# A new order of work for a sketched-attention kernel: PSUM banks named per operation, rows turned from PSUM

## The chip, the cores and the metric

The kernel runs on one core of a Trainium2 chip. A core has five engines, each with its own list of instructions in a fixed order: TensorE (PE, matrix products, with the loading of weights shown apart as PEld), VectorE (DVE), ScalarE (ACT), GpSimd (POOL) and SyncE (SP, which here only issues DMAs). They work side by side and wait for each other by semaphores. Data lies in SBUF (128 partitions); TensorE writes to PSUM (128 partitions, eight banks of 512 fp32 each). The metric is the device time in microseconds (us); lower is better. The kernel before takes 122.55 us, the median of three runs (122.51 to 123.03).

## The reference

Attention with sketched features, without a softmax, then a small network on each token. There are 4 batches, 4 heads, 1088 tokens and 32 elements per head:

```python
def phi(x):                       # 32 elements -> 8 x 8 = 64 features
    a = np.einsum('rd,bhsd->bhsr', S1, x)
    b = np.einsum('rd,bhsd->bhsr', S2, x)
    return np.einsum('bhsi,bhsj->bhsij', a, b).reshape(*x.shape[:-1], r * r)
q_p, k_p = phi(q), phi(k)
kv  = einsum('bhsf,bhsd->bhfd', k_p, v);  z = sum(k_p, axis=2)
num = einsum('bhsf,bhfd->bhsd', q_p, kv)
den = einsum('bhsf,bhf->bhs', q_p, z)[..., None] + 1e-06
x   = (num / den) laid out as (batch, token, 128)
xn  = (x - mean(x)) / sqrt(var(x) + 1e-06) * g_ln
out = x + maximum(xn @ w_ch1, 0) @ w_ch2          # 128 -> 512 -> 128
```

q, k, v are fp32; `S1`, `S2`, `g_ln`, `w_ch1` and `w_ch2` arrive as the 64-bit words of doubles and are turned to fp32 on the chip.

## The kernel before, in words

The order of everything is written by hand. `PROGRAM` is one string of operations with arguments; each calls a small function that issues one or a few instructions. What stands ahead in the string stands ahead on its engine too; waits between engines are put in from the data. A letter names the engine where there is a choice: V is DVE, A is ACT, G is POOL, S is SP. So `relu A B 0 2 2 4` is: ACT, PSUM bank B, chunk 0, slice 2 of the 512 hidden columns, token tiles 2 to 4.

PSUM is held in six tiles: two of two banks (X and Y, whose halves are A, B and C, D) and M, N, O, K of one bank each. Several operations always use the same one: `k_sum`, `k_sc`, `k_val`, `k_spr` use K, the packed features and the numerators use X and Y.

*Weights* (`w_ex` … `w_mul`, index 0 for S, 1 for w1, 2 for w2). Exponent, mantissa and sign of the double words are put together to fp32 by some eight elementwise steps, on DVE, ACT and POOL as the letter says. w1 goes in halves of 256 columns, w2 in one piece of 512. `fold` multiplies w1 by a matrix that centres and scales by `g_ln`, so that the product with x needs no mean; 1/sqrt(var) is applied at the end.

*Keys of a batch.* `ld S k b` loads them; `turn_g`, `turn_r` turn them on DVE so that elements lie on partitions. The features come directly as tokens by features (`k_dir`, nine 128x128 products, batches 0 and 1) or packed by features on partitions (`k_feat`) and are then turned by DVE (`k_tok`). `k_prod` forms the 64 products, `k_sum`, `k_zs`, `k_sc`, `k_sccp` the sums for the denominators; `k_val` multiplies by v (72 small products), and `k_vcp`, `k_spr`, `k_rcp` bring the result to the form that `num` needs.

*Queries of a batch.* Batch 0's are loaded in pieces by head and tokens (`ld_t`, `ld_tr`), turned by PE (`turn_p`) and copied (`turn_c`); `q_dir` gives features and denominators at once. Batches 1 to 3 use `turn_g`, `q_feat` and two `q_tok`. Then `q_ac`, `q_den`, `q_rec` (denominator and its reciprocal), `q_a2`, `q_prod` (64 products) and `q_turn` (DVE). In batch 0 the products read the features from PSUM (`q_ac0`, `q_b0`, `q_prod0`). All batches share one buffer of products for keys (`kp`), one for queries (`qp`) and one for turned query products (`qpT`).

*Rows and the network.* `num` (packed 32x32 products) gives the numerators with features on partitions, `num_cp` copies them to SBUF as `xT`: chunks 2b and 2b+1 of 512 tokens for batch b, and the 64 tokens over in chunks 8 (batches 0, 1) and 9 (batches 2, 3). `hid` (one of four slices of the hidden layer for 512 tokens), `relu` and `sec` (one tile of 128 tokens, four products) run on these. For statistics and the residual the rows are also needed with tokens on partitions: chunks 0, 1, 8 and 9 are turned by PE (`row_pe`, `row_cp`); chunks 2 to 7 by DVE in blocks of 32 (`row_turn`, one call per chunk, from the copy in SBUF), written to DRAM (`row_wr`) and read back in rows (`row_rd`). `st_bn`, `st_ag`, `st_pow` give 1/sqrt(var). At the end either DVE scales the `sec` and adds x in one instruction (`fin`), or ACT scales (`fin_a`, four tiles per call) and POOL adds (`fin_g`); `store` and `store_r` write to DRAM.

Line numbers that the views name, before: 254 `fill` (empty products that keep PE busy), 421 `turn_g`, 439 `turn_r`, 445 `turn_p`, 463 `k_dir`, 481 `k_feat`, 505 `k_sum`, 534 `k_val`, 569 `q_dir`, 602 `q_feat`, 611 `q_tok`, 649 `q_turn`, 663 `num`, 715 `row_pe`, 725 `row_turn`, 745 `st_bn`, 772 `hid`, 780 and 782 `relu`, 788 `sec`, 801 `fin`, 807 `fin_a`, 817 `fin_g`; 82, 84 and 87 are the helpers for copies and products, which many operations share.

Of the kernel before, what the change touches and what calls it, by code (L numbers as in the profile page):

```python
# [25 lines left out]
def kernel(  # L26
# [40 lines left out]
    XS = [ps.tile([P, 1024], F32, name=f"X{i}") for i in range(2)]  # L67
    M = [ps.tile([P, 512], F32, name=f"M{i}") for i in range(2)]
    PO = ps.tile([P, 512], F32, name="PO")
    KV = ps.tile([P, 512], F32, name="KV")  # L70
    banks = {"X": XS[0], "Y": XS[1], "M": M[0], "N": M[1], "O": PO, "K": KV,
             "A": XS[0][:, 0:512], "B": XS[0][:, 512:1024],
             "C": XS[1][:, 0:512], "D": XS[1][:, 512:1024]}

# [40 lines left out]
    @op  # L115
    def ld(eng, x, b, t0, t1):
        dst, src = rows_in[x]
        by[eng].dma_start(
            out=dst[b][:, D * t0 : D * t1],
            in_=bass.AP(src.tensor, src.offset + b * H * S * D + D * t0,  # L120
                        [[G * D, P], [1, D * (t1 - t0)]]),
        )

    @op
    def ld_u(eng, x, b, u0, u1):
        dst, src = rows_in[x]
# [315 lines left out]
    def turn_p(z, u0, u1):  # L442
        for u in range(u0, u1):
            n = P if u < 8 else 64
            pe.transpose(banks[z][:, P * (u - u0) : P * (u - u0) + n],
                         qt[0:n, P * u : P * (u + 1)], ident[0:n, 0:n])

    @op
    def turn_c(eng, z, u0, u1):
        n = P * (u1 - u0) - (64 if u1 == 9 else 0)  # L450
        copy(eng, qT[0][:, P * u0 : P * u0 + n], banks[z][:, 0:n])
# [9 lines left out]
    def k_dir(b, u0, u1, z):  # L461
        for u in range(u0, u1):
            pe.matmul(banks[z][:, KW * (u - u0) : KW * (u - u0 + 1)],  # L463
# [3 lines left out]
    def k_cp(eng, b, u0, u1, z):  # L467
        copy(eng, kf[b % 2][:, KW * u0 : KW * u1], banks[z][:, 0 : KW * (u1 - u0)])

    @op  # L470
    def k_prod0(u0, u1, z, k0):
        f, n, o = kf[0], (u1 - u0) * H, KW * (u0 - k0)
        times("V", _ap(kp, 0, P, H * F * u0, [[F, n], [R, R], [1, R]]),
              _ap(banks[z], 0, P, o, [[2 * R, n], [2, R], [0, R]]),
# [3 lines left out]
    def k_feat(b):  # L478
        for g in range(4):
            for hp in range(2):  # L480
                pe.matmul(
                    XS[0][32 * g : 32 * g + 32, 512 * hp : 512 * hp + TW],
# [6 lines left out]
    def k_tok(b):  # L489
        dve.transpose(_ap(kf[b % 2], 0, P, 0, [[32, 2], [KW, NU], [1, 32]]),  # L490
                      _ap(XS[0], 0, P, 0, [[512, 2], [32, NU], [1, 32]]))
# [9 lines left out]
    def k_sum(b):  # L501
        f = kf[b % 2]
        for u in range(NU):
            c = u % 4
            pe.matmul(
                KV[32 * c : 32 * c + 32, 128:160], _ap(f, 0, P, KW * u + 1, [[2, HR]]),
# [5 lines left out]
    def k_zs(b):  # L512
        dve.tensor_tensor(out=_ap(zT, 0, P, 0, [[R, H], [1, R]]),
                          in0=_ap(KV, 0, P, 128, [[R, H], [1, R]]),
# [15 lines left out]
    @op  # L530
    def k_val(b):
        for u in range(NU):
            for h in range(H):
                pe.matmul(
                    KV[D * h : D * h + D, 0:F],
# [6 lines left out]
    def k_vcp(eng, b):  # L542
        copy(eng, _ap(kvc, 0, P, 0, [[P, 2], [32, 4], [1, 32]]),
             _ap(KV, 0, P, 0, [[32, 2], [0, 4], [1, 32]]))

    @op
    def k_spr(b):
        for i in range(2):
            pe.transpose(KV[:, 256 + P * i : 256 + P * (i + 1)], kvc[:, P * i : P * (i + 1)], ident)

    @op
    def k_rcp(eng, b):
        copy(eng, kvr[b % 2], KV[:, 256:512])
# [13 lines left out]
    def q_dir(u0, u1, z):  # L567
        for u in range(u0, u1):
            pe.matmul(banks[z][:, W0 * (u - u0) : W0 * (u - u0 + 1)], qT[0][:, P * u : P * (u + 1)],
# [382 lines left out]
```

## Time and profile before

| | |
|---|---|
| median of three runs | 122.55 us (122.51 to 123.03) |
| span of the profiled execution | 120.9 us, 1.6 below the median |
| busy PE / PEld / DVE / ACT / POOL | 108.4 / 78.6 / 84.0 / 38.7 / 48.4 us |
| DMA | 13.31 MB: 9.31 read, 3.80 written |
| mean granted clock of PE | 0.993 |

The span runs from the first to the last instruction; the run times are measured from outside and also hold what lies around them. The views that follow give times in us from the span's start. In a group (`L421 DVE STREAM_TRANSPOSE qT<-qn 128x1024 …`) stand the line, the engine, the operation, the output and input tile with partitions x elements and the count; then the busy time of all, the mean of one in ns, and the idle time before them with what ended it. A table by stage gives busy time and number of instructions of PE, PEld, DVE, ACT and POOL for each stretch, then granted clock, share of DMA time and GB/s. The chain that ended last gives start, duration, engine, tile and line of each piece.

### The profile page before, as it was taken

The numbers are of one execution on the slowest core, as the hardware profiler recorded it, in microseconds if no ns is written. First come the engines' busy times: TensorE is split into PE (matmuls) and PEld (weight loads), VectorE is DVE, ScalarE is ACT, GpSimd is POOL, SyncE is SP. The second block draws the span as 40 slices with busy tenths as digits, with TensorE's granted clock in tenths as the row PEclk, the third lists the DMA queues.
The fourth block names the chain that finished last, engine by engine and source line by source line (L and its number), as shares of the span: only waits on it lengthen the run. The fifth ranks groups of instructions, "written<-read, shape, count | busy, mean of one in ns | idle before, by whom it ended". The sixth has DMA issues, their size and how long they took to land.

```text
span 120.9 us, 3295 instructions
## 1 busy us (share of the span) xinstructions
PE 108.4 (90%) x1347; PEld 78.6 (65%) x1347; DVE 84.0 (69%) x229; ACT 38.7 (32%) x100; POOL 48.4 (40%) x64
## 2 busy tenths in 40 slices
PE   5993999999898998998999799999979979979970
PEld 3382999848766773874665589766237946549970
DVE  2953308249999799899788999885993655391550
ACT  0062124224334358030701820264491500414000
POOL 6502242035839963301587903339643500006100
PEclk9999999999999999999999999999999999999997
DMA  3999799996000023011640120013640225300423
GB/s 110 262 315 245 139 251 233 272 249 182 0 5 5 0 62 131 0 26 68 203 147 0 43 87 0 5 66 118 188 159 0 87 92 173 91 17 13 161 87 108
DMA packets 15502, 13.31 MB, mean 110 GB/s; under 512 B 6528, under 2 KB 12416, under 8 KB 15488
## 3 DMA queue, kind: packets, MB, share of 16 engines
q1 hardware_dynamic: 11744, 9.54, 28.5%
q10 hardware_dynamic: 3712, 3.57, 9.7%
q8 instruction: 10, 0.16, 0.6%
q14 instruction: 4, 0.03, 0.1%
q0 software_dynamic: 32, 0.00, 0.0%
HBM read 9.31 MB, written 3.80 MB: 108 GB/s over the span
## 4 chain that ended last, share of the span: by engine, by line
PE 57%; DVE 18%; DMA 8%; ACT 6%; issue 4%; POOL 2%; ACTq 1%; DVEq 0%; POOLq 0%
PE X L772 8%; PE M L788 7%; PE X L663 5%; PE M L772 5%; DMA kn<-in_k_dram 4%; PE X L788 4%; DVE xh L725 4%; PE KV L788 3%; PE X L463 3%; DVE qpT L649 3%; DMA w_raw<-in_moe_w_ch_dram 3%; PE PO L788 3%; PE PO L772 2%; ACT xT L82 2%; PE M L463 2%
## 5 line engine op out<-in xcount | busy, mean ns | idle before, releaser
L758 POOL TENSOR_TENSOR rstd<-va,mhalf 128x4 f32<-128x4 f32 (+1 forms) x10 | 10.2, 1024 | 29.1 <-DVE va L752 28.1
L788 PEld LDWEIGHTS M<-w,hT 128*128 128x128 f32 x144 | 17.1, 192 | 5.1 <-issue 2.4
L788 PE MATMUL M<-w,hT 128*128 128x128 f32 x144 | 18.4, 278 | 1.1 <-ACT ob L807 0.6
L772 PE MATMUL X<-xT,w 128*128 128x512 f32 (+1 forms) x38 | 18.4, 586 | 0.8 <-DVE xr L84 0.8
L780 ACT ACTIVATE hT<-X 128x512 f32<-128x512 f32 (+2 forms) x18 | 9.9, 556 | 21.3 <-PE X L772 19.8
L87 POOL TENSOR_TENSOR kp<-kf 128x1280 f32<-128x1280 f32 (+3 forms) x7 | 13.1, 1883 | 4.9 <-ACT kf L82 3.2
L87 POOL TENSOR_TENSOR qp<-a,fq 128x1280 f32<-128x1280 f32 (+1 forms) x4 | 9.6, 2398 | 5.1 <-DVE a L87 5.0
L649 DVE STREAM_TRANSPOSE qpT<-qp 128x1280 f32<-128x1280 f32 (+2 forms) x9 | 11.0, 1227 | 0.5 <-POOL qp L87 0.4
L82 ACT COPY xT<-X 128x256 f32<-128x256 f32 (+1 forms) x13 | 6.1, 510 | 15.9 <-PE X L663 11.5
L772 PE MATMUL M<-xT,w 128*128 128x512 f32 (+1 forms) x20 | 9.0, 532 | 1.4 <-DVE hT L782 0.9
L254 PE MATMUL M<-ones 128*128 128x128 f32 (+2 forms) x16 | 8.7, 696 | 1.4 <-DVE m L202 1.4
L772 PEld LDWEIGHTS X<-xT,w 128*128 128x128 f32 x38 | 6.3, 190 | 4.7 <-issue 4.2
L663 PE MATMUL X<-qpT,kvr 32*32 32x288 f32 (+2 forms) x384 | 7.9, 332 | 1.1 <-issue 0.5
L725 DVE STREAM_TRANSPOSE xh<-xT 128x512 f32<-128x512 f32 x6 | 6.5, 1102 | 0.9 <-ACT xT L82 0.9
L772 PEld LDWEIGHTS M<-xT,w 128*128 128x128 f32 x20 | 3.4, 189 | 5.5 <-issue 1.9
L663 PEld LDWEIGHTS X<-qpT,kvr 32*32 32x32 f32 x384 | 4.7, 103 | 3.0 <-issue 1.0
L745 DVE BATCH_NORM_STATS2 st<-x 128x6 f32<-128x128 f32 x32 | 6.7, 274 | 0.0
L788 PEld LDWEIGHTS X<-w,hT 128*128 128x128 f32 x48 | 5.9, 192 | 1.0 <-issue 1.0
L788 PEld LDWEIGHTS KV<-w,hT 128*128 128x128 f32 x40 | 4.9, 191 | 2.2 <-ACT hT L780 1.7
L788 PE MATMUL X<-w,hT 128*128 128x128 f32 x48 | 6.2, 275 | 0.0
L772 PE MATMUL PO<-xT,w 128*128 128x512 f32 (+1 forms) x14 | 6.2, 522 | 0.0
L817 POOL TENSOR_TENSOR ob<-ob,x 128x512 f32<-128x512 f32 x4 | 5.1, 1282 | 2.5 <-ACT ob L807 2.5
(164 smaller groups left out, 195.2 us busy)
## 6 DMA issues: line engine op xcount, KB each, us to landing
out_dram<-ob SPq DMA_DIRECT2D x7, 256.0 KB, 2.9
vn<-in_v_dram SPq DMA_DIRECT2D x13, 128.0 KB, 4.8
qn<-in_q_dram SPq DMA_DIRECT2D x3, 544.0 KB, 5.6
xd<-xh SPq DMA_DIRECT2D x5, 256.0 KB, 2.3
kn<-in_k_dram ACTq DMA_DIRECT2D x2, 544.0 KB, 6.3
x<-xd SPq DMA_DIRECT2D x4, 256.0 KB, 2.7
kn<-in_k_dram SPq DMA_DIRECT2D x1, 544.0 KB, 7.5
w_raw<-in_moe_w_ch_dram SPq DMA_DIRECT2D x1, 512.0 KB, 6.3
```

Of the source, the lines that this page charges most:

```text
L82: act.copy(o, i)
L87: by[eng].tensor_tensor(out=o, in0=a, in1=b, op=ALU.mult)
L254: pe.matmul(M[0][:, 0:w], ones[:, 0:P], ones[:, 0:w], start=True, stop=True)
L463: pe.matmul(banks[z][:, KW * (u - u0) : KW * (u - u0 + 1)], kT[b % 2][:, P * u : P * (u + 1)], sk0, start=True, stop=True)
L649: dve.transpose(_ap(qpT, 0, P, 32 * u0, [[32, u1 - u0], [TW, 8], [1, 32]]), qp[:, H * F * u0 : H * F * u1])
L663: pe.matmul(XS[r // 2][D * h : D * h + D, o : o + w], kvr[b % 2][rows, DM * f + D * h : DM * f + D * h + D], qpT[rows, c : c + w], start=( ...
L725: dve.transpose(_ap(xh[slot(c)], 0, P, 0, [[32 * n, 4], [32, n], [1, 32]]), _ap(cols(c), 0, P, 0, [[1, 4], [P, n], [4, 32]]))
L745: dve.bn_stats(out=sts[slot(c)][:, 6 * t : 6 * t + 6], in_=row_ap(c, t))
L758: pool.tensor_tensor(out=rstds[slot(c)][:, 0:n], in0=vas[slot(c)][:, 0:n], in1=mhalf[:, 0:n], op=ALU.pow)
L772: pe.matmul(banks[z][:, 0:n], w1[:, P * j : P * (j + 1)], cols(c)[:, a : a + n], start=True, stop=True)
L780: act.activation(o, i, AF.Relu)
L788: pe.matmul(banks[z][:, DM * t : DM * (t + 1)], h[:, 512 * j + P * t : 512 * j + P * (t + 1)], w2[:, DM * j : DM * (j + 1)], start=(j == 0 ...
```

## The change

It does seven things.

1. PSUM is one tile of eight banks, and every operation names its bank or banks in `PROGRAM`.
2. Batch 0's features are direct, all others packed: batch 1's keys go through `k_feat` and `k_tok`. In batch 0's queries, `q_cp` now copies all 24 columns to SBUF, and the products are made from there, most of them on POOL, with the functions of the other batches.
3. `num` of batch 0 comes in two calls instead of three, and its columns lie as those of the other batches; `store` follows.
4. All of chunks 0 to 7 are turned by DVE and go through DRAM, each in two calls that read the numerators from PSUM instead of `xT`. PE turns chunks 8 and 9 alone.
5. k has two buffers instead of four, q two instead of three beside batch 0's.
6. `fin_a` takes one tile per call: 20 tiles go by `fin_a`, 14 by `fin`.
7. The order on all engines is new. Among others: `ld S q 1` and `turn_g q 1` stand ahead of the second half of `turn_g k 0`; w2 is loaded with w1 and converted mostly by ACT and POOL; `hid` of chunk 9 stands after the last `sec` of chunk 7.

```diff
-    XS = [ps.tile([P, 1024], F32, name=f"X{i}") for i in range(2)]
...
+    ALL = ps.tile([P, 4096], F32, name="ALL")
+    def bank(z, c0=0, c1=512):
+        return ALL[:, 512 * z + c0 : 512 * z + c1]
+    def pair(z, off, free):
+        return _ap(ALL, 0, P, 512 * z[0] + off, [[512 * (z[1] - z[0]), 2]] + free)
-    kn = const([P, G * D], F32, "kn", B)
+    kn = const([P, G * D], F32, "kn", 2) * 2
+    NAT = True
+    QDIR = {0}
+    qb = const([P, G * D], F32, "qn", 2)
+    qn = [qt, qb[0], qb[1], qb[0]]
     def num_cp(eng, b, i, u0, u1, *z):
-        o, w, r = (64 * i, 1, 32) if b == 0 else (2 * i, 4, 1)
+        copy(eng, _ap(xT[(2 * b + u0 // 4) % 4], 0, P, P * (u0 % 4) + 2 * i,
+                      [[1, 2], [P, n], [4, 32]]),
+             pair(z, 32 * u0, [[32, n], [1, 32]]))
-    through_dram = set((2, 3, 4, 5, 6, 7, ))
+    through_dram = {0, 1, 2, 3, 4, 5, 6, 7}
-    def row_turn(c):
+    def row_turn(c, i, *z):
         n = tiles(c)
-        dve.transpose(_ap(xh[slot(c)], 0, P, 0, [[32 * n, 4], [32, n], [1, 32]]),
-                      _ap(cols(c), 0, P, 0, [[1, 4], [P, n], [4, 32]]))
+        dve.transpose(_ap(xh[slot(c)], 0, P, 64 * n * i, [[32 * n, 2], [32, n], [1, 32]]),
+                      pair(z, P * (c % 2), [[32, n], [1, 32]]))
-    def fin_a(z, c):
-        for t in range(tiles(c)):
-            act.activation(...)
+    def fin_a(z, c, t):
+        act.activation(...)
-        runs = [[8 * DM, P]] if b == 0 else [[G * DM, 32], [8 * DM, 4]]
+        runs = [[8 * DM, 32], [256 * DM, 4]] if b == 0 and NAT else [[G * DM, 32], [8 * DM, 4]]
     PROGRAM = """
+    ld_s A 1; ld_s A 0; c_iota; c_ones; fill 4 256 7; c_small; ld A k 0 0 16; c_masks;
...
+    ld_t A 0 0 4; ld_w S 1 0 2; ld A k 0 16 34; w_low A 1 0 256; w_ex V 1 256 512;
...
+    s_heads G; turn_g k 0 0 2; ld_g; turn_r k 0; ld S q 1 0 34; turn_g q 1 0 4; ld_w S 2 0 4;
+    turn_g k 0 2 4; c_vpad 1; sk 6; sk_0 6; fill 1 256 7; k_dir 0 3 6 5; ld_t S 0 4 8;
...
+    sk_8 6; c_vpad 3; ld_v S 1 3; ld_v S 1 1; ld S k 2 0 34; sk_2 6; w_exf A 1 0 256; ld_v S 0 0;
+    c_pads 0; k_dir 0 6 9 4; ld_t S 3 0 4; ld_t A 2 4 8; ld_tr S; turn_r k 1; turn_p 3 0 4;
...
+    k_sccp A 0 1; c_rest; ld_t S 3 4 8; turn_p 7 4 8; q_dir 0 4 3; ld S k 3 0 34; turn_c A 7 4 8;
+    turn_c A 2 8 9; c_cg G; ld_vr S 0 0; q_cp A 0 4 3 0 24; q_ac G 0 0 4; q_dir 4 9 7;
...
+    k_sum 2 7; q_a2 G 0 0 4; q_prod G 0 0 2; q_a2 G 0 4 9; q_prod V 0 2 4; q_prod G 0 6 9;
+    q_turn 0 2; k_spr 0 3; q_prod G 0 4 6; q_feat 1 5 6 1 2; k_zs 2 7; q_turn 2 4; q_tok 1 0 5 6;
+    ld_vr S 1 0; k_rcp A 0 3; ld_vr S 2 0; q_turn 4 9; k_prod G 1 0 5; q_tok 1 1 1 2; turn_r k 3;
...
+    w_mant A 2 0 512; num 0 0 4 3 4 5 6; q_ac V 1 0 4; q_ac V 1 4 9; num_cp A 0 0 0 4 3 4;
+    k_feat 3 1 2; k_prod G 1 5 9; k_val 1 0 9 7; q_den 1 0 4; num_cp A 0 1 0 4 5 6;
+    hid 0 0 0 2 4; q_den 1 4 9; ld_vr S 3 0; q_rec 1 0 4; k_vcp A 1 7; q_rec 1 4 9; k_tok 3 1 2;
+    row_turn 0 1 5 6; ld_v S 3 0; hid 2 0 1 2 4; relu A 0 0 0 2 4; q_a2 G 1 0 4;
...
+    relu A 1 1 2 0 4; k_val 2 0 9 7; row_wr S 0; k_vcp A 2 7; row_wr S 1; w_e2 G 2 0 512;
+    k_sum 3 3; q_turn 4 9; q_ac G 2 0 4; ld_vr S 3 1; w_e3 V 2 0 512; w_add G 2 0 512;
+    relu A 4 1 0 0 4; row_rd S 0; k_zs 3 3; num 1 0 9 5 6 0 1; k_spr 2 7; k_sc 3 3;
+    relu V 2 0 1 0 2; hid 4 1 3 0 4; ld_v S 3 1; w_mul G 2 0 512; sec 2 0 1; st_bn 0;
...
+    sec 6 2 2; hid 3 3 0 0 4; k_vcp V 3 7; q_ac G 3 0 4; q_ac G 3 4 9; k_spr 3 7;
+    row_turn 4 1 4 5; sec 2 2 1; st_ag 3; num_cp A 2 0 0 4 0 1; row_turn 5 0 0 1; num_r V 2 0 1;
+    fin_g G 1; num_cp V 2 0 4 8 0 1; k_rcp V 3 7; relu A 3 3 0 0 4; store S 0 0 4; sec 7 2 0;
...
+    st_bn 7; fin 1 6 1; sec 1 7 1; sec 4 7 2; fin 5 6 3; sec 5 7 3; row_pe 9 2; st_ag 7;
+    st_pow 7; fin 0 6 0; hid 0 9 0 0 1; fin 6 6 2; fin 4 7 2; store S 6 0 4; fin 7 7 0;
+    hid 7 9 1 0 1; fin 1 7 1; row_cp A 9 2; fin 5 7 3; relu A 7 9 1 0 1; store S 5 0 4;
...
```

More of the change, by code (lines that the diff above doesn't have):

```diff
@@ L883 @@
-    row_rd S 2; fin_g G 0; relu A O 2 2 0 4; turn_g q 2 0 4; turn_g q 3 0 4; k_zs 3; q_feat 2;
-    hid N 3 0 0 4; sec M 1 1; k_spr 2; q_tok 2 1; q_tok 2 0; st_bn 1; st_ag 1; k_prod G 3 0 5;
-    sk_qq 3; c_vpad 3; st_pow 1; hid D 3 1 0 4; relu V D 3 1 0 4; hid B 2 0 0 4; q_ac V 2 4 9;
-    q_den 2 4 9; q_rec 2 4 9; q_a2 G 2 4 9; hid K 8 2 0 1; hid D 2 3 0 4; st_bn 3; q_ac G 2 0 4;
-    q_den 2 0 4; q_prod G 2 4 9; relu A B 2 0 0 4; hid B 8 1 0 1; hid C 3 2 0 4; k_sc 3;
-    k_sccp V 3; q_rec 2 0 4; relu A D 2 3 0 4; fin_a M 1; hid O 3 3 0 4; sec M 2 0; ld_v A 3 0;
@@ L889 @@
-    relu A C 3 2 0 4; q_a2 V 2 0 4; st_bn 2; relu A B 8 1 0 1; sec M 2 3; q_feat 3;
-    relu A O 3 3 0 4; relu A N 3 0 0 4; q_prod V 2 0 4; q_turn 4 9; q_tok 3 0; relu V K 8 2 0 1;
-    k_rcp V 2; hid N 8 0 0 1; relu V N 8 0 0 1; q_tok 3 1; q_turn 0 4; sec O 3 1; sec O 3 2;
-    sec M 2 2; sec M 2 1; hid K 8 3 0 1; sec O 3 0; num 2 0 9; ld_v S 3 2; sec O 3 3;
-    num_cp A 2 1 4 8; num_r A 2; relu A K 8 3 0 1; fin_g G 1; q_ac G 3 0 4; q_ac G 3 4 9;
-    store S 1 0 4; num_cp A 2 0 0 4; k_prod V 3 5 9; q_den 3 4 9; q_rec 3 4 9; st_ag 3; st_ag 2;
```

292 lines of the change are left out of this document (131 added, 161 removed).

## The prediction

> **What bounds the kernel now.** I read, in this order: the page's busy line, busy time by stage, the chain that ended last, the groups of instructions, the timeline of DVE and POOL. The stages (start:end, length; busy time of PE, PEld, DVE, ACT, POOL; granted clock, DMA share, GB/s):
>
> ```profile
> PE 108.4 (90%) x1347; PEld 78.6 (65%) x1347; DVE 84.0 (69%) x229; ACT 38.7 (32%) x100; POOL 48.4 (40%) x64
> 0.00:11.41 11.41, 8.11 (x18) 4.55 (x18) 5.51 (x26) 2.78 (x6) 3.61 (x19) 1.00 0.83 236
> 11.41:28.41 17.00, 17.00 (x182) 14.62 (x183) 7.42 (x20) 4.10 (x13) 4.74 (x12) 1.00 1.03 231
> 28.41:42.00 13.59, 12.72 (x359) 9.75 (x358) 13.05 (x24) 5.91 (x17) 10.75 (x9) 1.00 0.06 18
> 42.00:57.50 15.50, 14.48 (x234) 9.73 (x214) 14.51 (x32) 5.89 (x14) 5.17 (x3) 1.00 0.17 57
> 57.50:77.70 20.20, 19.51 (x245) 13.75 (x245) 18.33 (x49) 6.09 (x16) 10.78 (x13) 1.00 0.23 72
> 77.70:117.30 39.60, 36.63 (x334) 26.23 (x332) 24.83 (x83) 13.96 (x34) 13.34 (x12) 1.00 0.28 96
> ```
>
> PE looks full everywhere, but its records overlap. DVE tells the stages apart: until 28.4 the loads set the pace (DMA share 0.83 to 1.03, DVE under half busy); from 28.4 to 77.7 DVE is busy 45.9 of 49.3 us and paces everything; after 77.7 DVE is free a third of the time and PE paces. What PE really needs is read from the chain, whose pieces do not overlap (start, us, work):
>
> ```profile
> 4.96 5.39 DMA kn<-in_k_dram
> 11.41 1.54 PE X L463 x6
> 12.96 1.28 PE PO L463 x6
> 18.50 0.46 PE KV L505 x18
> 18.96 1.05 PE PO L445 x4
> 22.57 1.65 PE PO L569 x8
> 26.13 1.14 PE X L481 x16
> 27.27 1.14 PE KV L534 x72
> 28.41 0.59 PE M L445 x4
> 29.99 1.18 PE M L569 x10
> 33.20 0.51 PE M L772 x2
> 36.61 0.75 PE X L663 x44
> 38.96 0.44 PE X L715 x4
> 71.51 1.79 PE PO L788 x16
> 76.20 1.55 PE X L663 x63
> 100.22 0.86 PE M L772 x2
> 117.33 0.35 DVE ob L801
> ```
>
> The chain starts with a load of k and waits for the load and its turning until 11.41. In us: a `hid` of 512 columns 0.86, a `sec` 0.895, a `num` of a batch 1.55, `k_val` 1.14, three `k_dir` 1.28. Up to about 28 PE works at half rate though the granted clock reads 1.00: four `turn_p` take 1.05 at 18.96 and 0.59 at 28.41, a `q_dir` 0.41 at 22.57 and 0.24 at 29.99. After 77.7 the work left is 19 `sec` 17.0, hidden layers 14.6, `k_val` 1.14, `num` 1.55, small 0.5: 34.8 of 39.6, so 4.8 of waits.
>
> **The change, part by part.** PE loses nine `k_dir` (3.8; batch 1 now goes through one `k_feat`, 1.14), eight row transposes (0.88) and one narrow `num` call (0.75): 4.3 net, and some fills beside. That is no gain by itself: PE goes through its list in order, so only the wait that ends last counts. I walk along it.
>
> *Start.* SP issues w1 (two DMAs), k1, q1, w2; ACT S, k0, one piece of q. DVE now turns q1 ahead of the second half of k0, so the first `k_dir` waits for q1. DMAs to landing, and DVE's transposes:
>
> ```profile
> DMA to landing us min/median/max: 2.8/5.6/7.5
> L421 DVE STREAM_TRANSPOSE qT<-qn 128x1024 f32<-128x1024 f32 x3 | 3.5, 1201 | 0.0
> L421 DVE STREAM_TRANSPOSE kT<-kn 128x512 f32<-128x512 f32 x2 | 1.3, 681 | 0.0
> L439 DVE STREAM_TRANSPOSE kT<-kn 128x64 f32<-128x64 f32 x4 | 0.9, 227 | 0.0
> L649 DVE STREAM_TRANSPOSE qpT<-qp 128x1280 f32<-128x1280 f32 x4 | 6.0, 1504 | 0.0
> L611 DVE STREAM_TRANSPOSE fq<-X 128x576 f32<-128x576 f32 x6 | 4.4, 758 | 1.1 <-PE X L602 1.0
> L725 DVE STREAM_TRANSPOSE xh<-xT 128x512 f32<-128x512 f32 x6 | 6.5, 1102 | 0.9 <-ACT xT L82 0.9
> ```
>
> q1 is issued near 3.3 and lands 5.6 to 7.5 later; I take the late end, as 2.3 MB stand ahead of it (236 GB/s: 9.6), so 11.0. Turning q1 1.2, half of k0 0.68, `sk_0` 0.14: 13.0 against 11.41, a loss of 1.6.
>
> *Loads and `q_dir`.* PE does nine `k_dir` until 16.9, then waits for head 3's piece of q: SP issues it behind k2, which waits for k0 to be turned (13.0) and lands at 18.6 to 20.5. I take 19.4 for the piece. Then at half rate `turn_p` 1.05+0.3, `k_sum` 0.46, `k_feat` 1.14, `k_sc` 0.37, `turn_p` 1.05, nine `q_dir` 3.7: 27.5. PE ends `q_dir` 3.7 earlier than before (31.2), but DVE's q2 and the products wait behind it. w2's 0.5 MB, loaded late before, now delays k2 by some 2 us, which is in the 19.4.
>
> *Batch 0's queries* (DVE and POOL). From 27.5: copy 0.6, `q_ac`, `q_den`, `q_rec` 0.9; turn q2 1.2, `k_tok` 0.76 (31.0); POOL until 31.3; `q_prod` 0.65, two `q_turn` 1.4, `k_zs` 0.15, `q_tok` 0.76, `q_turn` 1.5, `q_tok` 0.76, small 0.6 (37.1). The next DVE work waits for POOL's `k_prod` of batch 1, until 37.3; then 0.6+1.1, `k_tok` 0.76, two half `row_turn`: no row has 128x256 out of PSUM. It lies between the 0.23 of a 128x64 and the 0.68 of a 128x512, on the line through the rows above (0.16 + n/960): 0.43, the value taken. Bounds for all sixteen: 3.7 to 10.9, sum 6.9, for the six of 1.1 that go (6.6). We are at 40.6. PE's first `hid` comes near 38, before it came at 33.2: this stage loses 5. If PE falls idle here long enough to go back to half rate, each `hid` costs 0.9 more until it recovers; the chain of before shows no such fall, so I price it at nothing and leave it to the range.
>
> *The middle, and the lock.* The rows that price POOL:
>
> ```profile
> L87 POOL TENSOR_TENSOR kp<-kf 128x1280 f32<-128x1280 f32 x3 | 7.2, 2390 | 0.0
> L87 POOL TENSOR_TENSOR kp<-kf 128x1024 f32<-128x1024 f32 x2 | 3.9, 1944 | 1.7 <-PE KV L534 1.7
> L322 POOL TENSOR_TENSOR mant<-mant,low 128x256 f32<-128x256 f32 x2 | 1.4, 725 | 11.3 <-ACT mant L300 11.3
> L817 POOL TENSOR_TENSOR ob<-ob,x 128x512 f32<-128x512 f32 x4 | 5.1, 1282 | 2.5 <-ACT ob L807 2.5
> L782 DVE TENSOR_SCALAR hT<-X 128x512 f32<-128x512 f32 x3 | 2.1, 688 | 1.9 <-PE X L772 1.8
> L745 DVE BATCH_NORM_STATS2 st<-x 128x6 f32<-128x128 f32 x32 | 6.7, 274 | 0.0
> 83.45 1.26 POOL L817 TENSOR_TENSOR ob<-ob,x 128x512 f32<-128x512 f32 x1
> 75.44 1.18 DVE L87 TENSOR_TENSOR kp<-kf 128x1024 f32<-128x1024 f32 x1
> 83.53 2.27 DVE L87 TENSOR_TENSOR qp<-a,fq 128x1024 f32<-128x1024 f32 x1 [1.45 <-POOL a L87]
> ```
>
> A DVE product that reads two SBUF tensors takes 1.18 alone; begun at 83.53 behind a POOL instruction that ended at 84.71, it took 2.27, that is the rest of POOL's instruction (1.18) and then about its own time. The change gives POOL more of such instructions: batch 0's products and w2's conversion raise its load from 48 to some 58. The Trainium skill, SBUF — State Buffer, "SBUF: two separate sides", says that VectorE and GpSimd share a port pair as an exclusive lock; by that rule every such meeting costs a wait, and the trace agrees in the one above (1.18 of waiting).
>
> DVE from 40.6 to the turned products of batch 2, by rows: `q_prod` 1.4, two `q_tok` 1.5, w2's exponent 0.6, three half `relu` 1.2, six `row_turn` 2.6, two `q_turn` 2.7, w2's sign 0.7, statistics of two chunks 2.6 (eight `st_bn` in 1.6, the rest `st_ag`), a copy 0.6, `k_prod` 1.2, `q_prod` 1.2, turn q3 1.2, two `q_turn` 2.7, small 1.9: 22.1. Waits for the lock, each the rest of the POOL instruction then running: 0.7, 0.4, 1.2, 0.3, 2.0, so 4.6 (bounds: 0, and 9 where each meets a whole one; I take the sum because the order puts DVE's five beside POOL's long products). That is 67.3; before, this `num` began at 76.2. The 9 us come from DVE's idle time until 28 (15.5 before), in which it now turns q1, k3 and q2 and does `k_tok`, and from w2's conversion, of which four of six steps leave DVE.
>
> SP issues 66 DMAs instead of 54, ACT 8 instead of 12. SP has no other work, but its list is in order: the write of chunk 1's rows waits for DVE (47) and holds the read of chunk 0's rows behind it, which lands near 51; DVE reaches `st_bn 0` 1.4 later. That slack is the cover of the two added round trips; without it they cost DVE what it lacks.
>
> *The end.* A `relu` 0.65 and `num` 1.4: 69.4; `k_val` 1.14: 70.5. PE then has 26 `sec` 23.3, hidden layers of chunks 3 to 7 17.2, of 8 and 9 1.8, `num` 1.55, small 0.5: 44.4. Banks that must be emptied first: 0.7 (`sec 7 2 0`, behind `k_rcp`). Chunk 9's hidden layer now stands after the last `sec` of chunk 7: its `relu` and the end of its `sec` are bare, 0.4. That is 116.0. ACT's single `fin_a` and DVE's `fin` are costed at nothing: the `hid` and `sec` between them cover them, and what they cost without that cover is the second rival. From the last PE piece to the span's end, before: 0.4 to the end of the last `fin` (117.7) and 3.2 for its store; I keep it: span 119.6. The median of the runs (122.55) is 1.6 above the profiled span (120.9): **121.2**.
>
> **Rivals.**
>
> *POOL becomes the bound (slower).* POOL's list between 38.8 and the end of `w_mul`: `k_prod` 4.3, `q_prod` 1.9, `q_a2` 1.0, `q_ac` 0.5, three steps on w2 at 512 columns 4.0 (between the 1.28 of an addition of that width and twice the 0.73 of 256), waits for DVE 2.6: 53. The first `sec` waits for it, and all of PE's list behind. Up to 67.3 PE has eight `sec`, four `hid` and a `q_feat` of 0.7 to do, 11.3, and some 1.4 of banks to wait for: 1.6 to spare. From `w_mul` at 54.6 on, each us of POOL is a us of time. Locks that cost POOL 4.6 more (what they cost DVE) put the end of `w_mul` at 57.6, 3.0 past that: 124.2. For it: the lock works both ways, and the converted w2 had no deadline this close before. Against: POOL is idle 60% now.
>
> *The end does not pack (slower).* Before, 4.8 of the last 39.6 us were waits (12%). The same share of 44.4 is 5.4, 4.3 more than I count: 125.5. For it: twenty single `fin_a` and fourteen `fin`, each holding a bank. Against: in the walk each bank but one that PE takes after 70 was emptied half a us or more before.
>
> *PE at full rate early (faster).* PE takes the full rate not at 28 but with its first steady work, the nine `k_dir`. By the two rates quoted, `turn_p` loses 0.9, `q_dir` 1.6, `k_feat` 0.5 by the same ratio: all that hangs on `q_dir` comes 3 earlier, 118.2. Against: the rows above show half rate still at 22.57, after 11 us in which PE was busy throughout. The Trainium skill, TensorE: Matmul & The Clock Gate, Part 1: The HAM clock gate, says that about 3.4 us of sustained work lift the gate; here the trace differs.
>
> *It does not do what it says.* The early loss (5 us on the first `hid`) is not won back before batch 2: 122.5, no change.
>
> **How the numbers follow.** My walk 0.46 (own range 119.0 to 123.6, the two sides of `row_turn`, of the landings and of half the lock), POOL 0.2, the end 0.14, full rate 0.13, no change 0.07. A measurement of this kernel tells about 0.5% (0.6 us) from no change: faster is under 121.9, slower over 123.2. Of my walk some 0.3 is faster, 0.08 the same, 0.08 slower; full rate is faster, no change the same, the other two slower: with a little rounding 0.44, 0.15, 0.41. The range reaches to both outer cases and leaves 0.2 outside: 117.4 to 125.6.
>
> **What would show it.** Right: first `k_dir` (line 448) near 13, last `q_dir` (554) near 27.5, first `hid` (757) near 38, first `sec` (773) near 53, `num` of batch 2 (648) near 67, PE's last piece near 116; POOL busy 57 to 60; two-input DVE work taking up to 2 us longer than alone. Wrong: q1 or head 3's piece landing elsewhere by 2 us, `num` of batch 2 ended by POOL instead of DVE, or gaps on PE after 70 above 3 us in all.

## The result, and the profile after

The changed kernel takes 118.28 us (median of four runs, 118.08 to 119.27); the ratio to the kernel before is 0.9645, with a 95% interval of 0.9593 to 0.9697. The profiled execution took 119.27, the slowest of the four; its span is 117.5, 1.8 below its own time. The ratios below compare the fast executions of each kernel, while a span is that of one profiled execution, and four of these (PE kept busy, k0 first, the product made to begin second, the repeat) were among the slow ones of their kernel. In the profile after: the busy line of the page, then busy time by stage (start:end, length; PE, PEld, DVE, ACT, POOL; granted clock, DMA share, GB/s).

```profile
PE 101.5 (86%) x1267; PEld 74.9 (64%) x1267; DVE 81.2 (69%) x232; ACT 38.5 (33%) x92; POOL 61.1 (52%) x75
12.90:28.30 15.40, 12.08 (x93) 10.40 (x96) 10.85 (x20) 3.50 (x11) 6.59 (x18) 1.00 0.94 218
28.30:40.40 12.10, 9.93 (x319) 6.36 (x317) 11.71 (x27) 3.55 (x8) 9.85 (x10) 0.90 0.34 91
40.40:53.90 13.50, 13.31 (x283) 8.63 (x280) 12.71 (x24) 7.59 (x17) 13.24 (x9) 0.96 0.29 92
53.90:67.00 13.10, 13.10 (x173) 10.17 (x175) 12.61 (x39) 6.04 (x16) 9.64 (x6) 1.00 0.25 82
67.00:91.40 24.40, 24.15 (x253) 16.64 (x252) 16.90 (x52) 8.57 (x22) 10.70 (x9) 1.00 0.22 77
```

POOL's busy time has risen from 48.4 to 61.1, and from 40.4 to 53.9 three engines are nearly full at once. Which of them paces is read from the chain that ended last (start, us, work):

```profile
2.56 10.33 DMA kn<-in_k_dram
13.16 1.13 DVE qT L414
20.33 1.38 PE ALL L431 x5
38.34 2.08 PE ALL L519 x72
40.42 2.03 PE ALL L757 x6
43.82 0.79 DVE fq L596
44.66 5.10 PE ALL L757 x16
54.05 6.41 PE ALL L773 x56
65.48 1.54 PE ALL L648 x57
107.52 3.65 PE ALL L773 x32
114.05 0.35 DVE ob L786
```

Up to 43.82 the chain runs over loads, PE's first products and DVE; from the `hid` at 44.66 (which waits for DVE's `q_tok 2`, line 596, to free its bank) it is PE, with one detour of 3 us and the last fall of 3 us over DVE. What PE waited for, kernel before from 28 on:

```profile
PE M L772 <- DVE hT L782: 0.9, 1, 0.9
PE X L772 <- DVE xr L84: 0.8, 1, 0.8
PE KV L788 <- ACT hT L780: 0.7, 1, 0.7
PE M L788 <- ACT ob L807: 0.6, 1, 0.6
...
PE M L788 <- DVE w L87: 0.5, 1, 0.5
```

and the changed kernel from 36 to 114, the whole answer:

```profile
PE ALL L466 <- DVE fq L596: 1.1, 1, 1.1
PE ALL L773 <- DVE kvr L84: 0.3, 1, 0.3
PE ALL L757 <- DVE fq L596: 0.2, 1, 0.2
```

The changed kernel is not ahead in the middle. Here are the records of `sec` up to 77.7 and behind it (eight to a `sec`), before and then after:

```profile
0.00:77.70 77.70, 15.12 (x121) 14.21 (x121) 1.00 0.45 118
77.70:118.00 40.30, 18.91 (x152) 17.94 (x152) 1.00 0.28 94
```

```profile
0.00:77.70 77.70, 12.62 (x104) 12.07 (x105) 0.98 0.52 145
77.70:115.00 37.30, 20.29 (x171) 19.55 (x169) 1.00 0.23 81
```

At 77.7 it is two `sec` (1.8) and one narrow `hid` of chunk 8 (0.22) behind, and only `k_val 3` (1.14) ahead. It wins behind this point. Of its last 39.6 us there the kernel before has 4.8 left beside PE's work (a subtraction; the first three lines of its list above and one more name 2.9 of it as waits). The changed one has 0.9 more to do and ends its last `sec` at 113.9, 36.2 later; the same subtraction leaves 0.5, and the list names no wait. So 4.8 less 0.5 less 0.9 is the 3.4 us that it wins. What makes it faster is that PE hardly lacks work or a bank after 44.7. Most of the waits of the kernel before are for a bank (M, X, KV) that another engine has to empty; which of the seven parts of the change took them away, no run separates, and the naming of banks was not tried alone.

### The profile page after: what moved, and what is told of

It is laid out like the page before. It is cut to its first block, busy times and chain, and to the rows that moved or that the text cites. A ratio compares the mean times of both kernels' runs of the same rounds, so it can differ in the third digit from the quotient of the medians.

```text
span 117.5 us, 3150 instructions
## 1 busy us (share of the span) xinstructions
PE 101.5 (86%) x1267; PEld 74.9 (64%) x1267; DVE 81.2 (69%) x232; ACT 38.5 (33%) x92; POOL 61.1 (52%) x75
## 4 chain that ended last, share of the span: by engine, by line
PE 65%; DVE 13%; DMA 13%; issue 3%; ACTq 1%; ACT 1%; POOLq 1%; SPq 0%; DVEq 0%
PE ALL L757 25%; PE ALL L773 23%; DMA kn<-in_k_dram 9%; PE ALL L648 4%; DMA vn<-in_v_dram 4%; PE ALL L519 4%; PE ALL L554 3%; PE ALL L431 2%; DVE qpT L634 2%; DVE qT L414 2%; DVE fq L596 2%; PE ALL L466 2%; DVE ob L786 1%; PE ALL L490 1%; DVE ac L87 1%
## 5 line engine op out<-in xcount | busy, mean ns | idle before, releaser
L773 PEld LDWEIGHTS ALL<-w,hT 128*128 128x128 f32 x272 | 31.6, 192 | 3.8 <-issue 1.4
L773 PE MATMUL ALL<-w,hT 128*128 128x128 f32 x272 | 32.9, 277 | 0.3 <-DVE kvr L84 0.3
L757 PE MATMUL ALL<-xT,w 128*128 128x512 f32 (+1 forms) x72 | 30.5, 564 | 0.2 <-DVE fq L596 0.2
L765 ACT ACTIVATE hT<-ALL 128x512 f32<-128x512 f32 (+2 forms) x28 | 13.8, 513 | 24.0 <-PE ALL L757 23.9
L757 PEld LDWEIGHTS ALL<-xT,w 128*128 128x128 f32 x72 | 13.0, 196 | 11.4 <-issue 7.3
L87 POOL TENSOR_TENSOR qp<-a,fq 128x512 f32<-128x512 f32 (+3 forms) x7 | 13.8, 1977 | 3.2 <-DVE a L87 3.0
L87 POOL TENSOR_TENSOR kp<-kf 128x1280 f32<-128x1280 f32 (+2 forms) x6 | 12.6, 2119 | 0.5 <-ACT kf L82 0.5
L767 DVE TENSOR_SCALAR hT<-ALL 128x512 f32<-128x512 f32 (+2 forms) x16 | 8.3, 531 | 5.3 <-PE ALL L757 5.3
L82 ACT COPY xT<-ALL 128x256 f32<-128x256 f32 x12 | 7.1, 643 | 8.6 <-PE ALL L648 4.4
L648 PE MATMUL ALL<-qpT,kvr 32*32 32x288 f32 (+2 forms) x320 | 7.8, 364 | 0.4 <-DVE qpT L634 0.3
```

Of the source, the lines that this page charges most:

```text
L82: act.copy(o, i)
L87: by[eng].tensor_tensor(out=o, in0=a, in1=b, op=ALU.mult)
L648: pe.matmul(bank(z[r], o, o + w)[D * h : D * h + D], kvr[b % 2][rows, DM * f + D * h : DM * f + D * h + D], qpT[rows, c : c + w], start=(f ...
L757: pe.matmul(bank(z, 0, n), w1[:, P * j : P * (j + 1)], cols(c)[:, a : a + n], start=True, stop=True)
L765: act.activation(o, i, AF.Relu)
L767: by[eng].tensor_scalar(out=o, in0=i, scalar1=0.0, scalar2=None, op0=ALU.max)
```

## Experiments

Two questions stood open: what sets the time, and why the forecast was 2.9 too high. The first theories: A, PE paces from 37.4 on; B, POOL's list up to `w_mul` does; C, DVE's list up to batch 2's numerators does.

**PE kept busy ahead of 38.**

```diff
- num 0 0 4 3 4 5 6;
+ fill 1 128 0; num 0 0 4 3 4 5 6; fill 3 256 0;
- fold 4 0 256;
+ fold 4 0 256; fill 1 256 0;
```

> The changed kernel with empty products on PE around 32 to 37.4 us (one of 128x256 after `fold 4 0 256`, one of 128x128 before batch 0's first `num`, three of 128x256 after it, all into a bank that nothing else holds then), so that PE does not fall idle ahead of 38. In the changed kernel the granted clock is 0.5 from 38.0 to 41.6, `k_val 1` takes 2.08 instead of 1.14 and three half `hid` 2.03 instead of 1.2. Theory A (PE paces from 37.4 to the end, 114, without gaps): the granted clock stays 1.00, PE comes to 44.7 some 1.7 earlier and keeps it, 116.6. Rival B (POOL's row of work up to `w_mul`, 53.9, and DVE's beside it pace until the first `sec`): the clock stays 1.00, but the first `sec` begins at 53.9 as before and the time stays 118.3. Rival C (it is the DVE order that leads to batch 2's numerators, 65.5): also 118.3, with `num` of batch 2 at 65.5.

The edit aims at this fall of the granted clock in the changed kernel (stages as above):

```profile
37.00:38.00 1.00, 0.56 (x16) 0.28 (x16) 1.00 (x5) 0.15 (x1) 1.00 (x1) 1.00 0.00 0
38.00:39.00 1.00, 1.00 (x38) 0.73 (x32) 1.00 (x3) 0.00 (x0) 0.53 (x1) 0.52 0.06 16
40.00:41.00 1.00, 1.00 (x18) 0.74 (x11) 1.00 (x4) 0.37 (x1) 1.00 (x3) 0.50 0.00 0
42.00:43.00 1.00, 1.00 (x37) 0.65 (x36) 1.00 (x1) 0.91 (x3) 1.00 (x2) 1.00 0.54 209
```

With the empty products the clock stays at 1.00, but (a row each of stages, PE's waits and the chain):

```profile
38.00:39.00 1.00, 1.00 (x37) 0.52 (x36) 1.00 (x5) 0.00 (x0) 0.13 (x1) 1.00 0.00 0
PE ALL L757 <- DVE fq L596: 0.9, 1, 0.9
44.28 5.10 PE ALL L757 x16
```

The ratio to the kernel before is 0.956 (0.949 to 0.964), the span 117.1. PE was earlier and then waited 0.9 for DVE's `q_tok`. Theory A falls in this form: before 44.66 PE is not what comes last. The 0.4 by which this `hid` came earlier is not the clock's either. DVE's first `q_tok` of batch 1 already began at 34.18 instead of 34.59, ahead of the fall, because two of DVE's products met POOL's in another order: 128x160 took 0.28 and 128x512 took 0.65, in the changed kernel 0.97 (at 28.95) and 1.05 (at 32.30). B and C do not fit, as the end moved with this `hid`; but 0.4 is less than the 1.0 by which the repeat below moved without an edit.

**k0 first.**

```diff
- ld A k 0 16 34;
+ ld S k 0 16 34;
- turn_r k 0; ld S q 1 0 34; turn_g q 1 0 4; ld_w S 2 0 4; turn_g k 0 2 4; ... sk_0 6;
+ turn_r k 0; ld S q 1 0 34; ld_w S 2 0 4; turn_g k 0 2 4; ... sk_0 6; turn_g q 1 0 4;
```

> The changed kernel, but the second half of k0 is issued by SP right after w1 (near 1.7 instead of 2.6), and DVE turns it ahead of q1. In the changed kernel it lands at 12.89, q1 is turned until 14.29, the first `k_dir` begins at 15.05 and the first `turn_p` at 20.33. If the order of the loads' issue decides: k0 lands near 9, first `k_dir` near 11, k2 is issued 3 earlier, `turn_p` near 18.3, and all behind it 2 earlier if PE paces to the end: 116.3. Rival (the bytes decide: DMA is busy 0.85 to 0.94 until 28): `k_dir` comes early, but `turn_p` stays within 0.5 of 20.3 and the time at 118.3.

Ratio 0.957 (0.952 to 0.962), span 117.2. `turn_p` came at 19.92 instead of 20.33, the `hid` at 44.27 instead of 44.66, the end 0.3 to 0.4 earlier. The chain now led over w2, which landed at 13.28 and held DVE's next step. So the rival (bytes, not one load) was nearer. What moved at 20 moved the end by about the same amount, but 0.4 is also less than the 0.8 by which the loads of the repeat moved without an edit.

**w2's conversion back on DVE** (`w_mant A`, `w_exf A`, `w_e2 G`, `w_add G`, `w_mul G` of w2 all become V).

> The changed kernel with five steps of w2's conversion back on DVE (mantissa, exponent to fp32, its shift, addition, product), as before the change; DVE gets 0.57+0.43+0.42+0.68+0.69 = 2.8 more, POOL loses 4.6 and ACT 1.5. Theory A (PE paces from 37.4): the mantissa's 0.6 delays `k_val 1`, the rest only where DVE comes later than PE, at batch 2's numerators, some 1.3: 118.9 to 120.2. Rival D (what DVE was relieved of is the gain of the change): all 2.8, 121.1. Rival B (POOL's list paces up to the first `sec`): the first `sec` comes earlier than 53.9 and the time falls below 118.

Ratio 0.989 (0.984 to 0.994): span 120.1. The `hid` came at 45.57, batch 1's `num` at 52.62 instead of 51.07. Of the 2.6 in span 0.5 is a later `turn_p` (20.88); some 2 are left, of the 2.8. By the ratio the time is 121.2, where D had 121.1. D is near; B falls.

**Chunks 0 and 1 turned by PE.**

```diff
- through_dram = {0, 1, 2, 3, 4, 5, 6, 7}
+ through_dram = {2, 3, 4, 5, 6, 7}
- row_turn 0 1 5 6; row_turn 0 0 3 4; row_turn 1 0 0 1; row_turn 1 1 6 7; row_wr/row_rd 0, 1
+ row_pe 0 3; row_cp A 0 3; ... row_pe 1 0; row_cp A 1 0
```

> The changed kernel with chunks 0 and 1 turned by PE again (four transposes and one ACT copy each, no DRAM trip). DVE loses four half `row_turn` (1.7), PE gets 0.88, ACT 1.2, SP loses four DMAs. Theory A (PE paces from 37.4): 0.9 slower, 119.2. Rival C (DVE's order up to batch 2's numerators paces): up to 1.7 faster, 116.6. If neither, 118.3.

Ratio 0.985 (0.980 to 0.990), span 119.1: slower than A's 0.9, although DVE was relieved. One reason is a row of DVE: the first step on w2, 0.73 in the changed kernel, here met POOL's `k_prod 2`:

```profile
45.71 2.35 DVE L274 TENSOR_SCALAR ex<-w_raw 128x512 uint32<-128x512 uint32 x1
```

After these four, theory E: DVE's list up to `q_tok 2` sets the `hid` of 44.66, and the end follows it one to one.

**Batch 0's products on DVE** (`q_prod G 0 …` become V).

> The changed kernel with the three products of batch 0's queries that POOL forms (128x512, 128x768, 128x512; 4.1 us of POOL between 28.7 and 34.3) on DVE. By DVE's 1.22 for 128x1024 they cost it 2.1. Theory E (after the first runs: DVE's row up to batch 2's `q_tok`, 44.6, sets when PE goes over to its stretch without gaps, and all of it moves the end one to one): the `hid` that begins at 44.66 begins 1.5 to 2.1 later and the time is 119.8 to 120.4. Rival F (DVE's waits for POOL's products, 0.4 at 32.3, 0.7 at 37.7, 1.4 at 40.9, cost as much as the products themselves): they go with POOL's products, and the `hid` stays at 44.7, the time at 118.3.

Ratio 1.022 (1.016 to 1.028), span 123.5. Neither theory priced this: 6 us for 2.1 of work. From the chain:

```profile
32.67 1.34 DVE qp L87 x2
34.01 2.20 issue
36.21 0.94 DVE qp L87
```

DVE's third product stood 2.2 behind POOL's two `k_prod 1` (31.01 to 35.74), w2's first step later took 2.46. F has it the wrong way round: the waits did not go with POOL's products, other meetings took their place. PE, after a wait of 4.2 for DVE, also ran at half rate from 38.6 to 45.4 (granted clock 0.50), and DVE waited 0.75 for the `q_feat` behind that; the clock's part in the later `hid` can hardly be more than this.

**A product made to begin second.**

```diff
- q_prod V 2 0 4; ... turn_g q 3 0 4;
+ turn_g q 3 0 4; q_prod V 2 0 4;
```

> The changed kernel with DVE's `q_prod 2 0 4` (128x1024, 1.22 at 58.96) behind `turn_g q 3`, so that it begins near 60.2, after POOL's product of 128x1280 has begun (58.99). In the changed kernel DVE's begins first: it takes 1.22, and POOL's takes 3.44 instead of 2.39. If whoever begins second waits for the rest of the other: DVE's takes 2.3 to 2.6, POOL's 2.4, and DVE's turned products are done near 65.1 instead of 63.98. Theory E (PE has no gap from 44.66 on; batch 2's `num` begins at 65.48, when PE has done what stands ahead, 1.5 after DVE): `num` stays at 65.5 and the time at 118.3. Rival C (DVE's order up to this `num` paces): 1.1 later, 119.4.

In the changed kernel (DVE, then POOL):

```profile
40.90 2.79 DVE L87 TENSOR_TENSOR qp<-a,fq 128x1280 f32<-128x1280 f32 x1
57.02 1.22 DVE L87 TENSOR_TENSOR kp<-kf 128x1024 f32<-128x1024 f32 x1
58.96 1.22 DVE L87 TENSOR_TENSOR qp<-a,fq 128x1024 f32<-128x1024 f32 x1
58.99 3.44 POOL L87 TENSOR_TENSOR qp<-a,fq 128x1280 f32<-128x1280 f32 x1 [0.49 <-DVE a L87]
```

With the order turned round:

```profile
62.11 2.34 DVE L87 TENSOR_TENSOR qp<-a,fq 128x1024 f32<-128x1024 f32 x1
60.98 2.39 POOL L87 TENSOR_TENSOR qp<-a,fq 128x1280 f32<-128x1280 f32 x1 [0.49 <-DVE a L87]
```

The two change roles, and the sum (4.66 and 4.73) stays. The Trainium skill, SBUF — State Buffer, "SBUF: two separate sides", says that whichever of the two starts first gets the shared ports for its whole instruction; here the trace agrees to within 0.15 us. For the time the run says less: ratio 0.973 (0.963 to 0.983), which overlaps that of the changed kernel, span 120.1. Of the 2.6, 0.95 is the later `hid` (45.61; the repeat of the changed kernel has 45.63), and some 0.75 is another meeting, `q_ac` of 128x160 at 53.57 with 1.36 instead of 0.31. Both stand ahead of the edit and are not its work. The other 0.9 arises from batch 2's `num` on, for which DVE was done at 67.1 instead of 64.0. That is near C's 1.1: at this `num` the slack of 1.5 on which E counted was used up.

**Loads in the order of need** (all pieces of batch 0's q right behind w1 and k0, then k1, q1, k2, v of batch 0, w2; on DVE q1, q2 and w2's first step further back).

> The changed kernel with the loads in the order in which PE needs them: w1, k0, all pieces of batch 0's q, k1, q1, k2, batch 0's v, w2, then the rest; DVE turns k0 first, q1, q2 and the first step on w2 stand further back in its list. In the changed kernel the first `turn_p` begins at 20.33 behind a piece of q issued at 15.80, the last `q_dir` ends at 28.26 and the `hid` of 44.66 follows 16.4 later. Theory E: `turn_p` begins near 14, `q_dir` ends near 22, then DVE's row is held by what lands late (q2, k3 near 30), so that the `hid` comes at 40 to 43 and the time is 114 to 117. Rival G (all bytes needed before 44 set the pace, not their order): `q_dir` ends early, but DVE waits for k2, k3, q2, v as long as before, and the time stays at 118.3 within 0.5.

Ratio 0.978 (0.972 to 0.985), span 118.0: no gain. DVE stood 4.1 for k2, which landed at 25.6; the `hid` came at 45.06. From the chain:

```profile
27.49 0.63 PE ALL L504 x2
30.07 1.14 PE ALL L466 x16
```

G is nearer than E: the loads are full until 28, and DVE waited for what landed late. But G is not shown. By the ratio the time is 119.9, 1.6 above the changed kernel's, which G did not forecast. And PE, after standing 3.5 for DVE, ran at half rate from 26.1 to 32.9 (granted clock 0.50): `k_feat 2` at 30.07 took 1.14 (0.65 in the run with PE kept busy), and DVE waited 2.8 for it. How early the `hid` would have come without this fall, no run shows.

**One part of the change alone, in the kernel before** (w2's five steps to ACT and POOL).

> The kernel before with one part of the change alone: w2's mantissa and exponent on ACT, its shift, addition and product on POOL (2.8 us off DVE, which is busy 45.9 of 49.3 us up to 77.7). If what DVE loses in that stretch is worth its size: batch 2's `num` 2 to 2.8 earlier than 76.2 and the time 119.8 to 120.5. If the gain needs the order too, because PE waits for something else next (4.8 us of waits after 77.7): 122.0 to 122.6. If POOL's steps (4.6, with what they wait) come too late for the first `sec` at 48: slower than 122.6.

Ratio 1.068 (1.061 to 1.076), the largest loss of all, some 8.4 us. The longest wait of PE:

```profile
PE M L788 <- POOL w L87: 6.8, 1, 6.8
```

The kernel before wants its first `sec` at 48, and POOL's `w_mul` stood behind its own products until 54.5. After this wait PE ran at half rate until 58.9, and the first 24 products of `sec` took 5.02 instead of 2.92. The changed kernel's `w_mul` is no earlier (53.88); it has put hidden layers there instead.

**The changed kernel again, and both starts together.**

> The changed kernel itself once more, on the chip of this set of runs, as the measure for the two below. All theories: 117.5 to 119.3, and the same waits on DVE: 1.3 to 1.4 at the product of 128x1280 near 41, none at those of 128x1024 near 57 and 59.

> The changed kernel with both the empty products on PE ahead of 38 and the second half of k0 loaded and turned ahead of q1. Alone, the one brought the `hid` of 44.66 to 44.28 though its loads landed 0.46 later, the other to 44.27. Theory E (this `hid` sets the end one to one, and waits for DVE's `q_tok`): the two add up to 0.8 to 1.2, and the time is 117.1 to 117.5. Rival: what the one wins the other wins too, 117.9.

Ratios 0.966 (0.958 to 0.974) and 0.961 (0.953 to 0.968), spans 118.5 and 117.3. For the changed kernel again:

```profile
21.09 1.38 PE ALL L431 x5
45.63 5.10 PE ALL L757 x16
38.00:39.00 1.00, 0.34 (x12) 0.28 (x16) 1.00 (x5) 0.38 (x1) 1.00 (x1) 1.00 0.00 0
PE ALL L757 <- DVE fq L596: 1.1, 1, 1.1
```

The same kernel's loads came 0.8 later than in its first profile, its `hid` 0.97, its end 1.0. Its times (118.45 to 121.73) went beyond the 119.3 expected, as did those of the kernel before in the same set (122.26 to 124.37). The waits on DVE were the same (2.79 at 41.87, 1.22 at 57.99 and 59.94). But here the clock did not fall at 38, without any empty product, and PE, which was earlier for it, waited 1.1 for `q_tok` instead of 0.2. So the fall took from PE only what PE would otherwise have waited, and this is the plainest support for E. With both edits the `hid` came at 44.42: they do not add up. PE waited 1.1 for `q_tok` again.

**POOL relieved** (`w_e2 G 2` becomes V).

> The changed kernel with one step of w2's conversion (the shift to the exponent's place, 1.92 on POOL at 48.3) on DVE, where it took 0.42 before the change. Rival B (POOL, busy 13.2 of 13.5 us from 40.4 to 53.9, paces the first `sec` by `w_mul`): the first `sec` begins up to 1.3 earlier than 53.95 and the time is 117.0 to 117.7. Theory E (PE has no gap around 53.95, so it does not wait for POOL, and DVE has 1.5 of slack ahead of batch 2's `num`): the first `sec` at 53.9 and the time at 118.3, within 0.4.

Ratio 0.974 (0.968 to 0.981), span 118.0. The first `sec` began at 54.5, not earlier, and DVE's step took three times its 0.42:

```profile
48.77 1.33 DVE L305 TENSOR_SCALAR ex<-exf 128x512 uint32<-128x512 f32 x1
```

`w_mul` was done at 53.5, a us ahead of this `sec`, and PE had stood 0.5 for DVE's `q_turn` instead. So POOL, though 98% busy, does not pace alone; it has no slack either, as in the changed kernel `w_mul` ends at 53.88 and the first `sec` begins at 53.94. E's own forecast (53.9, and 118.3 within 0.4) was missed too: by the ratio the time is 119.4.

**DVE's long product first** (the lines beside those of both starts together).

```diff
- row_turn 0 1 5 6; ... q_a2 G 1 0 4; row_turn 0 0 3 4; ... q_a2 G 1 4 9; ... q_prod V 1 4 9;
+ q_a2 G 1 4 9; q_a2 G 1 0 4; q_prod V 1 4 9; row_turn 0 1 5 6; row_turn 0 0 3 4;
```

> The kernel of the last set but one (empty products ahead of 38, second half of k0 first), and in it DVE's product of 128x1280 (2.79 near 40.7 behind POOL's product of 128x1024, 1.95) ahead of the two half `row_turn` of chunk 0, and POOL's scaling for it ahead of the other one, so that DVE begins before POOL's product does. If whoever begins second waits: DVE's takes 1.4 to 1.7, POOL's 1.95 up to 3.2. Theory E: the `hid` behind `q_tok` (44.42 there) comes 0.3 to 0.9 earlier, since the two `row_turn` now stand behind the product and hold the banks of PE's `q_feat`, and the end comes 72.9 after this `hid`: a span of 116.4 to 117.0, 118.1 to 118.8 in time. Rival: the wait comes back at DVE's next meeting with POOL (the step on w2 near 45, 0.73), and the span stays at 117.3.

Ratio 0.965 (0.958 to 0.972), span 117.8.

```profile
39.70 1.68 DVE L87 TENSOR_TENSOR qp<-a,fq 128x1280 f32<-128x1280 f32 x1
40.11 3.08 POOL L87 TENSOR_TENSOR qp<-a,fq 128x1024 f32<-128x1024 f32 x1
52.34 1.25 DVE L87 TENSOR_TENSOR ac<-fq 128x160 f32<-128x160 f32 x1
```

The wait of 1.1 went over to POOL as expected. But PE then waited 1.3 for the two `row_turn`, its `hid` came at 44.57, and a new meeting at 52.34 cost 0.9. The rival was right in kind, at another place than it named.

**What the runs give together.** The `hid` behind `q_tok 2`, the end of the span, and the difference:

| run | `hid` | span | between |
|---|---|---|---|
| changed kernel | 44.66 | 117.5 | 72.8 |
| the same again | 45.63 | 118.5 | 72.9 |
| busy ahead of 38 | 44.28 | 117.1 | 72.8 |
| k0 first | 44.27 | 117.2 | 72.9 |
| both | 44.42 | 117.3 | 72.9 |
| loads in order of need | 45.06 | 118.0 | 72.9 |
| long product first | 44.57 | 117.8 | 73.2 |
| POOL relieved | 44.67 | 118.0 | 73.3 |
| chunks 0, 1 by PE | 45.18 | 119.1 | 73.9 |
| product second | 45.61 | 120.1 | 74.5 |
| w2 on DVE | 45.57 | 120.1 | 74.5 |
| batch 0's products on DVE | 48.92 | 123.5 | 74.6 |

In the first six rows, where nothing behind the `hid` was changed, the end comes 72.8 to 72.9 later while the `hid` itself moves by 1.4: E. In the others more is between. Two of them (the long product first, batch 0's products on DVE) changed nothing behind the `hid` either; there a new meeting of DVE and POOL behind it (1.25 at 52.34, 2.46 at 49.46) is seen at the end. So E holds for this order as it stands, and says nothing of one that is changed behind the `hid`. No version is clearly faster than the changed kernel: the interval of the best ratio, 0.956 (0.949 to 0.964), overlaps that of its repeat, 0.966 (0.958 to 0.974).

## Why the prediction was right and wrong

The direction was right, and the time lies in the range (117.4 to 125.6); the size was not: 1.35 forecast, 4.27 measured. Point by point:

- *Start.* First `k_dir` 15.05, forecast 13.0. q1's landing did not hold it: k0's second half itself landed at 12.89, and only then were q1 (1.1) and this half turned. The loss was worth less than it looks, since head 3's piece of q came as forecast within a us (`turn_p` at 20.33) and the last `q_dir` ended at 28.26 (27.5).
- *Half rate.* Until 28 as forecast, so the rival of the full rate fell. That PE would fall back later was priced at nothing; it did, from 38 to 41.5, and the first `hid` began at 40.35 (38). It cost little: in the repeat, without the fall, the `hid` behind `q_tok 2` waited for DVE all the same, by 1.1 instead of 0.2.
- *Half `row_turn` from PSUM.* 0.43 on the line; the sixteen took 6.5 (6.9).
- *Batch 0 and up to `q_tok 2`.* DVE's second `q_tok` ended at 45.27; the walk has 40.6 + 1.4 + 0.7 + 1.5 = 44.2. A us late.
- *The step that failed: "Waits for the lock … so 4.6".* Behind `q_tok 2` the walk still had 3.9 of them (0.4, 1.2, 0.3, 2.0) and so 23.1 us until the turned products of batch 2. Measured: 18.7, done at 63.98. Step on w2, `k_prod`, scaling and `q_prod` took 0.69, 1.22, 0.33 and 1.22, that is, no wait; behind `q_tok 2` only the exponent's step at 45.19 waited, by 0.3 or somewhat more (0.73; 0.41 in the run with the long product first). DVE did wait ahead of it: 1.3 at the product of 40.90 (0.7 forecast), and 1.9 in three steps before that, for which the walk had nothing (0.97, 1.05 and, for two, 1.26 at 28.95, 32.30 and 37.65; 0.28, 0.65 and 0.50 in other runs). So the sum of the waits, 3.5 or somewhat more, was not far from 4.6, but most of them stood in another place. The mechanism was right, as two runs with the order turned round show; the mistake was to charge DVE for each meeting behind `q_tok 2`. In this order DVE begins first, and POOL pays: 3.44 instead of 2.39 at 58.99.
- *And then DVE was not the last.* `num` of batch 2 began at 65.48, when PE was through, 1.5 behind DVE. Forecast 67.3. That is 1.8 of the 2.1 by which the span was too long.
- *The end.* From this `num` to the end 52.3 forecast, 52.0 measured. The rival "the end does not pack" fell: no wait above 0.3. The time that I had read as won in the middle is won here.
- *POOL as the bound.* `w_mul` ended at 53.88 (53, with 54.6 as the limit). Nearly met: PE came to its first `sec` at 53.94. That POOL alone sets the time is refuted by the run that relieved it.
- *Span to time.* 1.6 forecast, 1.8 measured, but the profiled execution is 1.0 above the median. In the repeat a us came from the start, where its loads landed 0.8 later and PE stayed at half rate until about 30.5; whether that holds for the other executions is not shown.

So 121.2 − 118.28 = 2.9 is 2.1 of span (4.4 too much behind `q_tok 2`, less 1.1 too little ahead of it and 1.5 of PE, and 0.3 at the end) and 1.0 for the execution, less 0.2.

## What to carry to other kernels

Price a lock between two engines by who begins first at each meeting, and list the meetings in order; the sum of the other engine's busy time says nothing of it, and moving work between them makes new ones. Find the point from which the busiest engine has no gap, and look at what releases it there: here a us of DVE ahead of it was worth a us, and relieving POOL, 98% busy, gained none. After a long wait look at PE's rate too: in three runs it ran at half for 7 us behind one. A part of such a plan says little alone: one that cost some 3 us to undo cost 8 when put into the old order.

## What the runs showed of the hardware

- The lock also reaches DVE's work with one input from SBUF: w2's first step took 0.41, 0.73 and 2.35 in different runs, its shift 0.42 and 1.33, the longer the more of a POOL instruction was still to run. DVE's transposes kept their time (128x1024 took 1.19 to 1.25), and POOL's power of 128x4 (1.01 at 56.93) did not hold DVE's product at 57.02.
- PE's clock fell to half in the changed kernel from 38.0 to 41.5 after 2 us in which PE was busy 0.88. The busy time alone does not decide it: with the same 0.88 (loads in order of need) and in the repeat (1.19, then 0.34 from 38 to 39) it did not fall. In the six runs of the changed order without empty products whose full rate began near 28 it fell; in the three with them it did not, nor in the three whose full rate began later (about 30.5 in two, 32.9 in one). So the moment at which the full rate began seems to count beside the empty products; no run was made to settle this. The Trainium skill, TensorE: Matmul & The Clock Gate, Part 1: The HAM clock gate, gives about 3.4 us for the window in which it looks at activity; the length of the fall agrees.
- At the start PE runs at half rate until about 27 to 28.4 in most runs, also where its first `k_dir` came at 9.6 instead of 15.05. In the repeat and in the run with the product second it lasted until about 30.5; with the loads in order of need it ended at 22.7 and came back from 26.1 to 32.9. Four records read a granted clock of 0.50 in this stretch (w2's conversion on DVE, batch 0's products on DVE, loads in order of need, and w2's steps moved in the kernel before), the others 1.00, with the same 0.91 for four `turn_p`. Why the full rate comes so late was not found.
